# First batch of an mLSTM cell in natural chunks: compact state, fixed banks, gate work and weight joins at other slots

## The chip, the cores and the metric

One NeuronCore of a Trainium2 chip runs the whole kernel. The metric is the device time in microseconds (us) of one execution; the median over the runs is compared. Each engine works through its own queue strictly in order: the tensor engine (PE), VectorE (DVE), ScalarE (ACT), GpSimd (POOL), and SyncE (SP), which here issues every DMA.

## What is computed

An mLSTM cell over 4 batches, 8 heads, 768 tokens and head dimension 40, and behind it a Fourier mix over tokens and features, a layer norm and a ReLU MLP of width 1280.

```python
for t in range(S):                       # mLSTM, per batch and head
    m_new = np.maximum(f_gate[t] + m, i_gate[t])
    f_stab = np.exp(f_gate[t] + m - m_new)
    i_stab = np.exp(i_gate[t] - m_new)
    C = f_stab * C + i_stab * outer(v[t], k[t])
    n = f_stab * n + i_stab * k[t]
    y[t] = sigmoid(o_gate[t]) * (C @ q[t]) / np.maximum(np.abs(n @ q[t]), 1.0)
...
X = np.fft.fft(np.fft.fft(x, axis=1), axis=2)   # x: (batch, 768, 320)
u = x + np.real(X)
un = (u - mean(u)) / np.sqrt(var(u) + 1e-06)
out = u + np.maximum(un @ w_ch1, 0.0) @ w_ch2
```

## The kernel before

The recurrence is done in chunks of 128 tokens, six to a batch. For one chunk and all heads PE computes the scores k.q (`mlstm_scores`, L562), DVE multiplies them by exponential weights W (`mlstm_weigh`, L571), PE adds what the state so far gives (`mlstm_from_state`, L577, with the scaled queries qg of `mlstm_scale_q`, L523) to what the chunk itself gives (`mlstm_from_chunk`, L586), and the state C is decayed and added to (`mlstm_decay` L552 on POOL, `mlstm_to_state` L593 on PE, two copies in `mlstm_gather` L607 on ACT). The heads are copied to SBUF (`mlstm_heads`, L618), turned to rows (`mlstm_turn`, L638) and made into the layer's input x with the output gate `so`, after a tanh (`mlstm_tanh`, L634), in `mlstm_finish` (L743). Batch 0 is done so; batches 1 to 3 are done in half chunks of 64 tokens, from gate data that batch 0's time is used to prepare (`gates_of_halves`, L316, in steps: a maximum `nexts`, L326; copies into `keep`, L334 to 342; the exponentials G, L348; twelve stores M_d, L356; one store G_d, L358; later the exponentials K, L363).

The tokens are not in natural order. In every batch the chunks stand as START says, of which those in BACKWARDS run in reverse, so that chunk c and its partner in PAIRS hold tokens t and 768-t in one partition each. The first token of each half stands in a chunk of its own kind (SPECIAL), for which `mlstm_heads` moves a column.

Then, for a batch: a fold of each pair of row blocks (`mix_fold`, L828; sums and differences for the even and odd parts of both Fourier directions, in the pool `eo`, L837 to 849), products with the sequence tables ds_sb (`mix_seq`, L868; results pz, pzt), with the feature tables dd_sb (`mix_feat`, L932; results pu), the addition to x and its statistics (`mix_add`, L954), the centring of a block by ACT into `uc` (`mix_center`, L982), three transposes (`mix_turn`, L990; put or ph) and the MLP. The tables are loaded by `load_tables` (L464, L465: 1158 KB and 642 KB).

The weights come as 64-bit floats and are turned into fp32 in pieces (`Piece`, L411): take on DVE (L435, L437), convert on ACT (L442 e, L443 m), join on DVE (L449, L451, L455).

The order of all this is written out by hand: `at(slot, phase, fn, args)` enters a call in a plan, and `run` emits the calls by slot and phase (EVAC, FILL, MAIN, FILL_PE are 0, 1, 2, 3). That order is the order of each engine's queue. `plan_mlstm` (L764) places chunk c of batch 0 from slot 3c on, `plan_halves` (L784) the later batches, `plan_mix` (L1028) the mix; `gates` (L147) ends with the places of the gate steps, and the lists `when` and `early` place the weight pieces and the loads.

PSUM has eight banks of 2 KB a partition: ps_m with four (`turn` says which comes next), ps_s with two for scores and ps_h with two for the results ph, pc, px and pt in batch 0; later batches use ps_s and ps_h as two 2-bank tiles.

```python
    early = [(3, mlstm_load, 3), (3, mlstm_load_o, 2), (4, mlstm_load, 4), (5, mlstm_load_decay, 3),
             (5, mlstm_load_decay, 4), (6, None, 2), (7, mlstm_load_o, 3), (7, mlstm_load, 5),
             (11, mlstm_load_decay, 5), (11, mlstm_load_o, 4), (12, load_tables, None),
             (14, mlstm_load_o, 5)]
```

Of the kernel before, what the change touches and what calls it, by code (L numbers as in the profile page):

```python
# [37 lines left out]
COL = (0, L + 1, 2 * L + 2)  # L38
LAST = 2 * L + 1
# [4 lines left out]
BACKWARDS = (2, 4, 5)  # L44
# [13 lines left out]
def kernel(  # L58
# [30 lines left out]
    ps_s, ps_h = (ps_early.enter_context(tc.tile_pool(name=n, bufs=2, space=PSUM)) for n in ("ps_s", "ps_h"))  # L89

    turn = iter("3210321032120312031230123102112310231023102310231")
# [7 lines left out]
    rest = const.tile([L, 2 * L], FP, name="rest")  # L99
# [16 lines left out]
    C_bufs = [const.tile([L, NP, L], FP, name=f"C{n}") for n in range(3)]  # L116
    states = [t.rearrange("p n t -> p (n t)")[:, i * 2 * L:(i + 1) * 2 * L] for t in C_bufs for i in range(2)]
    x_bufs = [const.tile([L, NT, DM + 2], FP, name=f"x{n}") for n in range(2)]

    s_last = const.tile([L, NFF // 2 * L], FP, name="s_last")  # L120
    Cd_bufs = [s_last[:, n * NP * D1:(n + 1) * NP * D1].rearrange("p (n m) -> p n m", m=D1) for n in range(2)]
    hT_bufs = []
# [18 lines left out]
    def idle_products(n, first=False):  # L141
        pw = bank("pi", [L, 2 * L]) if first else ps_s.tile([L, 2 * L], FP, name="pi", tag="ps")
        for i in range(n):
            nc.tensor.matmul(pw, rest[:, 0:L], rest, start=True, stop=True, skip_group_check=True)


    def gates(gp):  # L147
# [3 lines left out]
        hT_bufs.extend(gp.tile([L, NP, L + 1], FP, name=f"h{n}") for n in range(2))  # L151
# [6 lines left out]
        M = gp.tile([L, NT, L], FP, name="M")  # L158
# [6 lines left out]
        ident_b, later_b = (gp.tile([L, L], BF, name=n) for n in ("ident_b", "later_b"))  # L165
# [4 lines left out]
        idle_products(3, True)  # L170
        mlstm_load(0, 0)
        make_identity(nc, ident)
        nc.gpsimd.memset(later_b, 0.0)
# [8 lines left out]
        nc.vector.memset(M[:, 0:2], 0.0)  # L182
        for t in C_bufs:
            nc.scalar.copy(out=t.rearrange("p (two n) t -> p two (n t)", two=2),
                           in_=rest.unsqueeze(1).to_broadcast([L, 2, 2 * L]))
# [8 lines left out]
        for t in hT_bufs + Cd_bufs + alone:  # L194
            nc.gpsimd.memset(t, 0.0)
# [21 lines left out]
        def spread_max(b, c, h0):  # L217
# [5 lines left out]
            k.M.append(bank("pM", [L, NP, L]))  # L223
            nc.tensor.matmul(k.M[-1], ident_b, later_b.unsqueeze(1).to_broadcast([L, NP, L]), start=True, stop=False,
                             skip_group_check=True)
            for h in range(h0, h0 + NP):
                bh = b * H + h
                w, x = (ident[:, bh:bh + 1], M[:, c, :]) if c < 2 else (sel[:, bh:bh + 1], M3[:, c, :])
# [3 lines left out]
        def parts(s):  # L232

            m, rest_ = M[0:BH, s], shift[:, s]
# [5 lines left out]

        def spread_decay(b, c):
            k = chunks[b, c]
            k.G = bank("pG", [L, NP, L])
            for h in range(H):
                r, bh = slice(h % 2 * 64, (h % 2 + 1) * 64), b * H + h
                nc.tensor.matmul(k.G[r, h // 2, :], ident[:, bh:bh + 1].to_broadcast([L, 64]), g[:, c, :],
                                 start=True, stop=True)
# [5 lines left out]
        def decay(s):  # L253
            for c in range(s.start, s.stop):
                nc.scalar.activation(out=g[0:BH, c], in_=M[0:BH, c], func=AF.Exp, scale=-1.0, bias=m_in[:, c])

        def columns(s, j):
            pt = ps_h.tile([L, NT, BH], FP, name="pt", tag="ph")
# [6 lines left out]
        maxima(first, M_INIT)  # L265
        pt = columns(first, 0)
# [34 lines left out]
        def decays():  # L301
            dec = gp.tile([BH, BH // 2, NT], FP, name="dec")
            nc.vector.tensor_tensor(out=dec[:, :, 1:],
                                    in0=g[0:BH, 1:, L - 1].unsqueeze(1).to_broadcast([BH, BH // 2, NT - 1]),
# [1237 lines left out]
```

## Time and profile before

| what | us |
|---|---|
| median of 3 runs (401.59, 401.64, 402.67) | 401.64 |
| profiled execution | 402.01 |
| its span, first to last instruction | 400.3 |
| chunks of batch 0 on PE (from_state of chunks 1, 2, 3, 4, 5) | 18.26, 23.37, 28.39, 34.62, 38.18 |
| last fold of pair 0 of batch 0 ends (DVE) | 47.82 |
| first from_state of batch 1 | 76.19 |

The mean granted PE clock over the span is 0.991. The rest of the span, from 76 to 400, is batches 1 to 3, their mixes and the four MLPs, with PE nearly always busy. A row of the timeline reads: start, length of a group of like instructions, engine and line, operation, output tile and input tiles, sizes, count, and in brackets the idle time of the engine before it and what ended it.

### The profile page before, as it was taken

The page shows a single profiled execution, that of the slowest core. Times are in us where ns is not written, and L with a number is a line of the kernel's source. Part 1 is how long each engine was busy: PE and PEld are TensorE (multiplying, and loading weights), DVE is VectorE, ACT ScalarE, POOL GpSimd, SP SyncE. Part 2 cuts the span into 40 slices and gives each one's busy share as a digit, 9 for nine tenths or more (in the row PEclk, how much of TensorE's full clock was granted, in tenths as well). Part 3 has the DMA queues.
Part 4 walks back from the last instruction along what each step waited for, and adds up shares of the span by engine and source line. Part 5 has one row for each costly group of instructions (what it writes and reads, how often), then busy time and mean ns, then how long its engine had stood idle before and what let it go on. Part 6 is the DMA issues. An engine that isn't in the chain of part 4 may idle for free.

```text
span 400.3 us, 10816 instructions
## 1 busy us (share of the span) xinstructions
PE 384.4 (96%) x4318; PEld 281.2 (70%) x4318; DVE 277.3 (69%) x670; ACT 178.2 (45%) x513; POOL 135.4 (34%) x231
## 2 busy tenths in 40 slices
PE   8999896999889999999999998999999999999996
PEld 6888453556557777755459898856579997556996
DVE  8776963689799546879774688678853785336652
ACT  6978844677533232563542214564440023454000
POOL 6654521676836432263251304562300000020000
PEclk9999996999999999999999999999999999999999
DMA  7987498288776143455000814520000000000000
GB/s 225 295 240 257 104 241 201 73 234 239 239 208 157 61 129 99 155 169 174 7 0 2 215 51 143 182 77 5 0 0 18 18 34 33 2 0 1 34 34 34
DMA packets 22767, 43.97 MB, mean 110 GB/s; under 512 B 3492, under 2 KB 11388, under 8 KB 22588
## 3 DMA queue, kind: packets, MB, share of 16 engines
q1 hardware_dynamic: 22716, 43.27, 36.8%
q8 instruction: 34, 0.56, 0.5%
q14 instruction: 17, 0.14, 0.1%
HBM read 39.16 MB, written 4.10 MB: 108 GB/s over the span
## 4 chain that ended last, share of the span: by engine, by line
PE 73%; DVE 18%; issue 3%; ACT 2%; POOL 2%; DVEq 0%; POOLq 0%; ACTq 0%
PE po L1274 21%; PE pm L1145 14%; PE po L1218 8%; PE pm L1150 5%; PE pu L952 3%; PE ph L549 3%; PE ps L549 3%; PE pm L1082 2%; PE pz L907 2%; DVE so L758 2%; PE put L999 1%; DVE x L761 1%; PE pzt L907 1%; DVE h L1154 1%; PE pM L229 1%
## 5 line engine op out<-in xcount | busy, mean ns | idle before, releaser
L1224 DVE SCALAR_TENSOR_TENSOR x<-po,rstd,x 128x160 f32<-128x160 f32 (+1 forms) x69 | 27.2, 394 | 38.9 <-PE po L1274 36.3
L1154 DVE TENSOR_TENSOR h<-h,pm 128x384 f32<-128x384 f32 x60 | 30.6, 550 | 26.6 <-PE pm L1150 12.1
L545 POOL TENSOR_SCALAR_AFFINE_SELECT W<-W 64x512 f32<-64x512 f32 x36 | 28.1, 780 | 39.3 <-ACT W L520 38.1
L1145 PE MATMUL pm<-uT,w_sb 128*128 128x384 f32 x90 | 37.8, 507 | 0.2 <-DVE uT L1133 0.2
L698 POOL TENSOR_TENSOR C<-C,decB 128x164 f32<-128x164 f32 x33 | 17.9, 542 | 56.2 <-DVE C L705 54.8
L520 ACT ACTIVATE W<-W,colT 128x64 f32<-128x64 f32 x144 | 36.6, 336 | 0.0
L1218 PE MATMUL po<-w_sb,h 128*128 128x320 f32 x120 | 34.1, 435 | 0.0
L1023 POOL TENSOR_TENSOR t<-rstd 128x6 f32<-128x6 f32 x12 | 4.2, 353 | 81.4 <-DVE v L1017 80.9
L530 POOL TENSOR_TENSOR qg<-qk,Gb 128x512 f32<-128x512 f32 x21 | 28.5, 1357 | 7.5 <-DMA Gb<-G_d 7.5
L1082 PE MATMUL pm<-uT,w_sb 128*128 128x384 f32 x80 | 29.9, 509 | 0.0
L1274 PE MATMUL po<-T,S 128*128 128x160 f32 x180 | 28.0, 302 | 1.1 <-DVE x L1224 1.1
L1218 PEld LDWEIGHTS po<-w_sb,h 128*128 128x128 f32 x120 | 22.3, 190 | 9.1 <-issue 0.6
L1274 PEld LDWEIGHTS po<-T,S 128*128 128x128 f32 x180 | 25.4, 190 | 2.7 <-DVE x L1224 1.3
L1150 PE MATMUL pm<-uT,w_sb 64*128 64x384 f32 x120 | 26.3, 511 | 0.4 <-DVE h L1154 0.4
L1274 PE MATMUL po<-w_sb,h 128*128 128x160 f32 x180 | 26.3, 300 | 0.0
L1274 PEld LDWEIGHTS po<-w_sb,h 128*128 128x128 f32 x180 | 25.2, 190 | 1.5 <-DVE x L1224 0.3
L1145 PEld LDWEIGHTS pm<-uT,w_sb 128*128 128x128 f32 x90 | 15.4, 189 | 13.8 <-DVE h L1154 5.9
L1201 ACT ACTIVATE h<-h 128x384 f32<-128x384 f32 x45 | 23.1, 520 | 3.0 <-DVE h L1154 3.0
L988 ACT ACTIVATE uc<-x 128x384 f32<-128x384 f32 x24 | 14.5, 614 | 20.2 <-DVE x L980 20.2
L705 DVE TENSOR_TENSOR C<-C,ps 128x164 f32<-128x164 f32 x33 | 10.5, 317 | 18.0 <-PE ps L549 15.3
L1150 PEld LDWEIGHTS pm<-uT,w_sb 64*128 64x128 f32 x120 | 12.8, 185 | 12.8 <-issue 8.2
L1004 ACT COPY uT<-put 128x384 f32<-128x384 f32 x21 | 9.6, 476 | 26.9 <-PE put L999 26.8
(242 smaller groups left out, 859.5 us busy)
## 6 DMA issues: line engine op xcount, KB each, us to landing
kvt<-in_kv SPq DMA_DIRECT2D x24, 336.0 KB
qk<-in_qkT SPq DMA_DIRECT2D x48, 160.0 KB
raw<-in_w SPq DMA_DIRECT2D x10, 640.0 KB
Gb<-G_d SPq DMA_DIRECT2D x42, 128.0 KB
W<-M_d SPq DMA_DIRECT2D x36, 128.0 KB
so<-in_o SPq DMA_DIRECT2D x24, 160.0 KB
out<-x SPq DMA_DIRECT2D x24, 160.0 KB
ds_sb<-in_dft_s SPq DMA_DIRECT2D x1, 1158.0 KB
```

Source lines behind the costliest of these rows:

```text
L520: nc.scalar.activation(out=k.W[:, h, :], in_=M, func=AF.Exp, scale=-1.0, bias=colT[:, c, 0, b * H + h:b * H + h + 1])
L530: nc.gpsimd.tensor_tensor(out=k.qg[:, :, t], in0=k.qk[:, 0, :, t], in1=k.Gb[:, :, t], op=OP.mult)
L545: nc.gpsimd.affine_select(out=W, in_=W, compare_op=OP.is_ge, fill=0.0, base=base, pattern=[[0, H], [-1 if back else 1, LH]], channel_multi ...
L549: nc.tensor.matmul(out, w, x, start=start, stop=True, skip_group_check=True)
L1082: nc.tensor.matmul(k.pm[i], w1_block(ch, f // 2 * 2 + i), u[2 * ch], start=(ch == 0 and not ahead), stop=(ch == 1 and ahead), skip_group_c ...
L1145: nc.tensor.matmul(bank, w, u, start=start, stop=True, skip_group_check=True)
L1150: nc.tensor.matmul(bank, w1_rest(i)[rows], mlp_u(gr, 1)[rows], start=False, stop=True, skip_group_check=True)
L1154: nc.vector.tensor_tensor(out=h, in0=h, in1=bank, op=OP.add)
L1201: nc.scalar.activation(out=h, in_=h, func=AF.Relu, scale=-1.0)
L1218: nc.tensor.matmul(k.po[m], hidden(gr, f)[:, i * L:(i + 1) * L], w2_sb[:, f, :], start=(f == 0), stop=(f == NFF - 1))
L1224: nc.vector.scalar_tensor_tensor(out=u, in0=po, scalar=k.rstd[:, c:c + 1], in1=u, op0=OP.mult, op1=OP.add)
L1274: nc.tensor.matmul(po, a[:, f], w[:, f], start=start and f == 0, stop=f == half - 1, skip_group_check=True)
```

## The change

- In batch 0 the chunks hold tokens in natural order (reversed in BACKWARDS, now 0, 3 and 4). `_first()` orders the host arrays. The reversed chunks use a mask `later_r`, and the running maxima in the order of the queries are kept beside the natural ones as Mq (`queries()`, three ACT copies). Row 0 of chunks 0 and 1 and of 3 and 4 are exchanged afterwards (`mlstm_rows`, three one-partition copies each).
- The head order of batch 0 becomes that of the others (head h in half h // 4).
- The state of batch 0 is compact: 41 columns for each of four heads in a half of the partitions. `mlstm_from_state` is 8 products of 40x64 in four quadrants of PE for 4 of 128x128. POOL decays it in place in one operation, and DVE adds the chunk's part (`mlstm_add`) where four products with the identity and two ACT copies did it. The decayed copy in s_last goes.
- Banks: heads of batch 0 lie in one tile of two banks (also pt and pzt); pc, px and pM have fixed banks.
- The steps of `gates_of_halves` go from slots 15 to 22 to slots 6 to 23: `nexts` 10, M_d's stores 11, G's exponentials in two halves at 13 and 16. Weight piece 0 is joined in three parts at slots 7, 10 and 13, piece 1 is taken, converted and joined at 16 to 18.5, and piece 2 at 31 to 33 with its load at 15.
- The folds' ends are one addition each instead of an addition and a copy; `eo` has two buffers; the slots of batch 0's folds, sequence and feature products move, and `mix_center` of two blocks stands right behind their `mix_add`.

```diff
-COL = (0, L + 1, 2 * L + 2)
-LAST = 2 * L + 1
+COL = (0, L, 2 * L)
+LAST = 3 * L
...
-BACKWARDS = (2, 4, 5)
+BACKWARDS = (0, 3, 4)
...
-    ps_s, ps_h = (ps_early.enter_context(tc.tile_pool(name=n, bufs=2, space=PSUM)) for n in ("ps_s", "ps_h"))
-
-    turn = iter("3210321032120312031230123102112310231023102310231")
+    ps_s = ps_early.enter_context(tc.tile_pool(name="ps_s", bufs=2, space=PSUM))
+    first_heads_ps = ps_early.enter_context(tc.tile_pool(name="ps_h", bufs=1, space=PSUM)).tile([L, 2, 4 * L], FP, name="hb")
+
+    turn = iter("3210321223102112310231023102310231")
...
+        def queries():
+
+            x, y = M[0:BH, 3], Mq[0:BH, 3:5]
+            nc.scalar.copy(out=y[:, :, 1:], in_=bass.AP(tensor=x.tensor, offset=x.offset + L - 1,
+                                                        ap=[list(x.ap[0]), [L, 2], [-1, L - 1]]))
+            nc.scalar.copy(out=y[:, :, 0:1], in_=M[0:BH, 3:5, 0:1])
+            nc.scalar.copy(out=Mq[0:BH, 5], in_=M[0:BH, 5])
...
-        def decays():
...
+        def decays(step):
+            if step == 0:
+                dec = late["dec"] = gp.tile([BH, BH // 2, NT], FP, name="dec")
+                for c, at_ in ((1, L - 1), (3, 1)):
+                    nc.vector.tensor_tensor(out=dec[:, :, c:c + 2],
+                                            in0=g[0:BH, c:c + 2, at_].unsqueeze(1).to_broadcast([BH, BH // 2, 2]),
+                                            in1=spread_sb[:, L:].unsqueeze(2).to_broadcast([BH, BH // 2, 2]), op=OP.mult)
+            else:
+                pd = late["pd"] = bank("pd", [L, BH // 2, NT - 2])
+                nc.tensor.matmul(pd, spread_sb[:, 0:L], late["dec"][:, :, 1:NT - 1], start=True, stop=True)
...
+            elif step == 20:
+                less, starts, nexts = (late[n] for n in ("less", "starts", "nexts"))
                 nc.vector.tensor_tensor(out=nexts[:, 1:], in0=M[0:BH, 0:NT - 1, L - 1:L], in1=a[:, 1:, 0:1], op=OP.max)
-                nc.gpsimd.tensor_copy(out=starts, in_=M[0:BH, :, 0:L:LH])
                 for out, x in ((less[:, :, 0:1], M[0:BH, :, LH:LH + 1]), (less[:, 0:NT - 1, 1:2], nexts[:, 1:]),
                                (less[:, NT - 1:, 1:2], M[0:BH, NT - 1:, L - 1:L])):
                     nc.gpsimd.tensor_scalar(out=out, in0=x, scalar1=-1.0, scalar2=None, op0=OP.mult)
                 nc.gpsimd.tensor_tensor(out=late["between"], in0=starts, in1=less, op=OP.add)
...
+            elif step == 21:
+                nc.gpsimd.tensor_copy(out=W[:, 0:4:3, LH:LH + 1], in_=late["nexts"][:, 1:5:3])
                 nc.gpsimd.tensor_copy(out=W[:, 4, LH:LH + 1], in_=late["nexts"][:, 5])
             elif step == 2:
-                nc.scalar.activation(out=late["between"], in_=late["between"], func=AF.Exp)
-                for c in range(NT):
-                    for i in range(2):
-                        t = slice(i * LH, (i + 1) * LH)
-                        nc.scalar.activation(out=G[:, c, t], in_=W[:, c, t], func=AF.Exp, scale=-1.0,
-                                             bias=late["starts"][:, c, i:i + 1])
                 nc.sync.dma_start(out=sp_sb, in_=first_heads)
                 for b in range(1, B):
                     for hip in range(2):
...
                             slot = slice(b * H + i * NP, b * H + (i + 1) * NP)
                             nc.sync.dma_start(out=M_d[:, i ^ hip, slot].rearrange("c p t -> p c t"),
                                               in_=W[rows, :, i * LH:(i + 1) * LH])
-                nc.sync.dma_start(out=G_d[:, H:].rearrange("c p t -> p c t"), in_=G[H:BH])
+            elif step in (10, 11):
+                if step == 10:
+                    nc.scalar.activation(out=late["between"], in_=late["between"], func=AF.Exp)
+                for c in range(*(((0, NT // 2), (NT // 2, NT))[step - 10])):
+                    for i in range(2):
+                        t = slice(i * LH, (i + 1) * LH)
+                        nc.scalar.activation(out=G[:, c, t], in_=W[:, c, t], func=AF.Exp, scale=-1.0,
+                                             bias=late["starts"][:, c, i:i + 1])
+                if step == 11:
+                    nc.sync.dma_start(out=G_d[:, H:].rearrange("c p t -> p c t"), in_=G[H:BH])
...
-        at(1, FILL + 0.2, parts, last)
+        at(1, FILL + 0.2, parts, slice(2, 3))
+        at(2, FILL + 0.6, queries)
+        at(4, FILL + 0.2, parts, slice(3, NT))
         at(5, FILL_PE + 2.1, spread_decay, 0, 2)
         for c in range(2, NT):
             for h0 in (0, NP):
                 at(3 * c - 1, FILL_PE + 2, spread_max, 0, c, h0)
         at(2, FILL + 0.5, columns_late)
         at(4, FILL - 0.4, decay_late)
-        at(4, FILL + 0.5, decays)
-        at(5, FILL - 0.5, decays_out)
+        at(4, FILL + 0.5, decays, 0)
+        at(5, FILL_PE + 2.05, decays, 1)
+        at(6, FILL - 0.05, decays_out)
         at(7, FILL + 0.5, clear, fe[:, :, NC:PAD], fe[:, :, PAD + HALF_D - 1:], fe_odd[:, NC:])
-        for n, (s, phase) in enumerate(((15, FILL + 0.75), (16, FILL + 0.75), (18, FILL + 0.75), (19, FILL + 0.75),
-                                        (18, FILL + 0.8), (19, FILL_PE + 0.5), (20, FILL + 0.75),
-                                        (21, FILL_PE + 0.5), (22, FILL + 0.75))):
+        for n, s, phase in ((0, 6, FILL + 0.75), (1, 8, FILL + 0.75), (20, 10, FILL + 0.02), (21, 10, FILL + 0.85),
+                            (2, 11, FILL + 0.75), (10, 13, FILL + 0.3), (4, 14, FILL + 0.8), (11, 16, FILL + 0.1),
+                            (5, 17, FILL_PE + 2.5), (3, 18, FILL + 0.1),
+                            (6, 18, FILL + 0.05), (7, 22, FILL_PE + 4.5), (8, 23, FILL + 0.2)):
             at(s, phase, gates_of_halves, n)
...
-            k.Cd = Cd_bufs[c % 2]
-            for hip in range(2):
-                r, m = slice(hip * 64, hip * 64 + D), slice(hip * 64, hip * 64 + D1)
-                d = decB[r, b * NP:(b + 1) * NP, c].unsqueeze(2).to_broadcast([D, NP, D1])
-                nc.gpsimd.tensor_tensor(out=k.Cd[r], in0=k.C[0][r, :, m], in1=d, op=OP.mult)
+            nc.gpsimd.tensor_tensor(out=halves_state(k.C[1]), in0=halves_state(k.C[0]),
+                                    in1=decB[:, 0:NP, c].unsqueeze(2).to_broadcast([L, NP, D1]), op=OP.mult)
...
-        k.ph = ps_h.tile([L, NP, L], FP, name="ph", tag="ph")
-        if c > 0:
-            for p in range(NP):
-                nc.tensor.matmul(k.ph[:, p, :], k.C[0][:, p, :], k.qg[:, p, :], start=(p == 0), stop=False,
-                                 skip_group_check=True)
+        k.ph = first_heads_ps[:, :, 0:2 * L].rearrange("p hip (m t) -> p hip m t", t=L)
+        for p in range(0, NP, 2) if c > 0 else ():
+            for hip, i in TILES:
+                r, n = slice(hip * 64, hip * 64 + D), (p + i) * D1
+                product(k.ph[half(i), hip, p // 2, :], k.C[0][r, n:n + LH], k.qg[r, p + i, :], p == 0)
 
     def mlstm_from_chunk(b, c):
         k = chunks[b, c]
+        for h in range(H):
+            hip, p = h // NP, h % NP
+            product(k.ph[half(p % 2), hip, p // 2, :], k.v[:, h * D1:h * D1 + LH], k.W[:, h, :], c == 0 and p < 2)
+
+    def mlstm_to_state(b, c):
+        k = chunks[b, c]
+        k.pc = bank("pc", [L, NP, D1], 2 if c > 0 else 1)
         for p in range(NP):
             for hip in range(2):
...
-                for hip in range(2):
-                    r = slice(hip * 64, hip * 64 + D)
-                    nc.tensor.matmul(k.pc[r], ident[:, r], k.Cd, start=False, stop=True, skip_group_check=True)
...
+                h = hip * NP + p
+                product(k.pc[half(hip), p, :], k.k[:, h * D:h * D + LH], k.vw[:, h, :], p == 0)
...
+    def mlstm_heads(b, c):
+        k = chunks[b, c]
+        k.hT = hT_bufs[c % 2]
+        nc.scalar.copy(out=k.hT.rearrange("p (hip m) t -> p hip m t", hip=2), in_=k.ph)
+
...
+    def mlstm_add(b, c):
+        k = chunks[b, c]
+        if c == 0:
+            nc.vector.tensor_copy(out=halves_state(k.C[1]), in_=k.pc)
         else:
-            for r in (slice(hip * 64, hip * 64 + D1) for hip in range(2)) if c == 0 else (slice(0, L),):
-                nc.scalar.copy(out=hT[r, :, 0:L], in_=ph[r])
+            nc.vector.tensor_tensor(out=halves_state(k.C[1]), in0=halves_state(k.C[1]), in1=k.pc, op=OP.add)
...
+    def mlstm_rows(b, c, part):
+
+        spare, x = s_last[0:1, 0:DM], xs[b][0:1, :, 0:DM]
+        if part == 0:
+            nc.scalar.copy(out=spare, in_=x[:, c - 1])
+        elif part == 1:
+            nc.vector.tensor_copy(out=x[:, c - 1], in_=x[:, c])
+        else:
+            nc.scalar.copy(out=x[:, c], in_=spare)
+
+    def plan_mlstm(b):
         for c in range(NT):
-            s = s0 + stride * c
+            s, end = 3 * c, c == NT - 1
             if c > 0:
                 at(s, FILL, mlstm_exp, b, c, 0)
                 at(s + 1, FILL - 0.5, mlstm_exp, b, c, NP)
-                at(s - 1 if c == NT - 1 else s, FILL_PE + (2.05 if c == NT - 1 else 2), mlstm_scores, b, c)
+                at(s, FILL_PE + (3.5 if end else 2), mlstm_scores, b, c)
             at(s, FILL, mlstm_scale_v, b, c)
             at(s if c == 2 else s + 1, FILL + 0.1, mlstm_scale_q, b, c)
-            at(s + 2, FILL, mlstm_decay, b, c)
-            end = c == NT - 1
-            at(s + 1 if end else s + 2, FILL - 0.4 if end else FILL, mlstm_weigh, b, c)
+            at(6 if c == 1 else s + 2, FILL, mlstm_decay, b, c)
+            at(s + 1, FILL + (0.2 if end else -0.4), mlstm_weigh, b, c)
             at(s + 2 if end else s + 3, FILL_PE, mlstm_from_state, b, c)
             at(s + 2 if end else s + 3, FILL_PE + (2 if end else 3), mlstm_from_chunk, b, c)
-            at(s + 3, FILL_PE + 3, mlstm_to_state, b, c)
-            at(s + 3 if end else s + 4, FILL, mlstm_gather, b, c)
-            t, x = ((8, 9), (11, 12), (13, 14), (16, 16.5), (17, 18), (18, 20))[c]
-            at(t, FILL_PE + (2.5 if c < 4 else 1), mlstm_turn, b, c, c < 4)
-            at(x, FILL + 0.05, mlstm_finish, b, c)
+            if not end:
+                at(s + 3, FILL_PE + 3, mlstm_to_state, b, c)
+                at(s + 4, FILL - 0.3, mlstm_add, b, c)
+            at(*((17, FILL_PE + 2.6) if end else (s + 4, FILL - 0.27)), mlstm_heads, b, c)
+            at(*((16, FILL + 0.02) if end else (s + 4, FILL - 0.25)), mlstm_tanh, b, c)
+            t, phase = ((5, 2.5), (8, 2.5), (11, 2.5), (14, 2.5), (16, 0.5), (17, 2.8))[c]
+            at(t, FILL_PE + phase, mlstm_turn, b, c)
+            t, phase = ((6, 0.3), (9, -0.3), (12, -0.3), (15, -0.3), (16.5, 0.4), (18.5, 0))[c]
+            at(t, FILL + phase, mlstm_finish, b, c)
+        for c, part, t, phase in ((1, 0, 7, 0.3), (1, 1, 9, -0.2), (1, 2, 10, -0.1), (4, 0, 16, 0.01), (4, 1, 16.5, 0.45),
+                                  (4, 2, 18, 0)):
...
+                at((17, 18.5, 18.5)[j], FILL + (0.1, 0.2, 0.3)[j], mix_fold, b, p)
+                s, phase = ((17, 3), (19, 3), (22, 4))[j]
+                for i, part in enumerate(((1,), (0,)) if j == 1 else ((0, 1),)):
+                    at(s, FILL_PE + phase + 0.1 * i, mix_seq, b, p, part)
+                at(*((18, FILL_PE + 0.2) if j == 0 else (s, FILL_PE + phase + 0.2)), mix_tail, b, p)
+            else:
+                at(x_done[j] + (b > 1 and j == TG - 1), FILL + 0.5 if b < 2 else FILL_PE + 0.2, mix_fold, b, p)
+            if b > 0 and j == 0:
...
-            at(t, FILL + 0.1, mix_center, b, c)
+            at(*((a, FILL + 0.25) if b == 0 and c in (4, 2) else (t, FILL + 0.1)), mix_center, b, c)
...
-    eo_p = pool("eo", 1)
+    eo_p = pool("eo", 2)
...
-    when = [((2, 0.7), (4, 0.5), (6, 0.6)), ((11, 0.7), (13, 0.7), (22, 0.6)), ((29, 0.7), (30, 0.7), (32, 0.6))]
+    when = [((2, 0.7), (4, 0.5), None), ((16, -0.2), (18, 0.08), (18.5, 0.6)), ((31, 0.7), (32, 0.7), (33, 0.6))]
     when += [((s, 0.7), (s + 1, 0.7), (s + 2, 0.6)) for s in range(33, 52, 3)]
     pieces = w1_pieces + w2_pieces
     for n, (w, p) in enumerate(zip(when, pieces)):
         if n > 2:
             at(when[n - 2][2][0] + 1, FILL + 0.7, p.load)
-        for (s, phase), fn in zip(w, (p.take, p.convert, p.join)):
-            at(s, FILL + phase, fn)
+        for t, fn in zip(w, (p.take, p.convert, p.join)):
+            if t:
+                at(t[0], FILL + t[1], fn)
+    for part, s in enumerate((7, 10, 13)):
...
-             (5, mlstm_load_decay, 4), (6, None, 2), (7, mlstm_load_o, 3), (7, mlstm_load, 5),
-             (11, mlstm_load_decay, 5), (11, mlstm_load_o, 4), (12, load_tables, None),
+             (5, mlstm_load_decay, 4), (7, mlstm_load_o, 3), (7, mlstm_load, 5),
+             (11, mlstm_load_decay, 5), (11, mlstm_load_o, 4), (12, load_tables, None), (15, None, 2),
...
+def _first():
+
+    t = np.arange(S).reshape(NT, L)
+    for c in BACKWARDS:
+        t[c, 1:] = t[c, :0:-1].copy()
+    return t
...
```

## The prediction

> **What bounds the kernel now.** Four views, in this order. The page's busy shares: the tensor engine (PE) is busy 96% of the span, so over most of it any time won must be a shorter PE stream or a PE wait removed. The engines' busy time by stretches (columns: stretch, its length, then busy time with instruction count of PE, PEld, DVE, ACT and POOL, then granted clock, DMA share, GB/s) shows where PE is not full:
>
> ```profile
> PE 384.4 (96%) x4318; PEld 281.2 (70%) x4318; DVE 277.3 (69%) x670; ACT 178.2 (45%) x513; POOL 135.4 (34%) x231
> ```
>
> ```profile
> 20.00:38.00 18.00, 17.96 (x272) 15.03 (x268) 11.69 (x28) 14.22 (x48) 9.93 (x18) 1.00 0.91 274
> 38.00:53.00 15.00, 13.68 (x82) 8.39 (x83) 11.37 (x31) 11.91 (x45) 5.29 (x10) 1.00 0.47 123
> 53.00:64.00 11.00, 7.32 (x32) 3.77 (x31) 9.94 (x25) 6.08 (x14) 2.38 (x3) 0.96 0.94 234
> 64.00:76.00 12.00, 12.00 (x97) 6.71 (x97) 3.52 (x7) 6.92 (x21) 5.62 (x9) 0.75 0.56 143
> ```
>
> In 20 to 38 (the chunks of batch 0) PE is the bound. In 53 to 64 it is idle 3.7 us, and from 64 to 76 it is full but at a granted clock of 0.75. The timeline names the idle time, PE first, then ACT:
>
> ```profile
> 58.20 2.20 PE L1082 MATMUL pm<-uT,w_sb 128*128 128x384 f32 x6
> 63.94 0.90 PE L999 MATMUL ph<-ident,uc 128*128 128x128 f32 x3 [3.54 <-ACT uc L988]
> ...
> 60.97 0.83 ACT L442 ACTIVATE e<-e,ebias 128x640 uint32<-128x640 uint32 x1 [2.83 <-DVE e L435]
> 61.71 0.72 ACT L443 ACTIVATE m<-m 128x640 f32<-128x640 uint32 x1
> 62.33 1.05 ACT L520 ACTIVATE W<-W,colT 128x64 f32<-128x64 f32 x4
> 63.29 0.60 ACT L988 ACTIVATE uc<-x 128x384 f32<-128x384 f32 x1
> ```
>
> PE waits 3.54 us for a centred row block, `uc`, whose ACT instruction stands behind a weight's conversion (e, m), and that one waits for DVE. Last, SP's queue, which issues every load in order, and the DMA rate while the Fourier tables fly:
>
> ```profile
> 28.36 0.33 SPq L464 DMA_DIRECT2D ds_sb<-in_dft_s  x1
> 28.92 0.33 SPq L465 DMA_DIRECT2D dd_sb<-in_dft_d  x1
> 30.32 0.33 SPq L513 DMA_DIRECT2D so<-in_o  x1
> 30.69 0.43 SPq L350 DMA_DIRECT2D sp_sb<-in_heads  x1
> 40.08 4.17 SPq L356 DMA_DIRECT2D M_d<-keep  x12
> ```
>
> ```profile
> 28.00:33.00 5.00, 5.00 (x76) 4.38 (x75) 3.04 (x9) 3.60 (x13) 3.17 (x5) 1.00 1.07 258
> 33.00:38.00 5.00, 4.96 (x72) 4.00 (x69) 2.43 (x7) 4.73 (x15) 3.14 (x9) 1.00 0.88 346
> 38.00:45.00 7.00, 6.08 (x48) 4.11 (x48) 6.30 (x20) 6.17 (x24) 4.32 (x8) 1.00 0.07 20
> ```
>
> The reader is to see that tables and the last output gate (`so`) are issued ten microseconds before the twelve stores of M_d, and that those take SP 4.17 us. The tables are 1158 KB and 642 KB (page, part 6, and its longer form).
>
> **The chunk loop.** Before, from_state of chunks 2 and 3 starts at 23.37 and 28.39 on PE: 5.0 us a chunk. Removed: the four identity products L605 (31.68 to 32.05: 0.38). Smaller: from_state takes 0.98 from its start to that of the scores (28.39 to 29.37); in its compact form it is 16 instructions of 40x64. The trace has 32 of nearly that form for batch 1 (L549, 1.13 for all), so half of that, 0.5 to 0.57, saves 0.4. Bounds: nothing saved to 0.5 saved. The join of C on PE becomes one DVE add (0.32, the row L705 of the same size) and the two ACT copies (0.61) go. That is 5.0 less 0.78, and 0.1 back for from_chunk and the 64-wide keys: 4.3 us a chunk. ACT and DVE have the room (14.2 and 11.7 of 18 busy). POOL does one decay instead of two.
>
> **What eats it.** Three waits, each from the order of the queues.
> (1) The product of the decays, pd, stands in PE's queue after the scores of chunk 1, and its factor `dec` on DVE behind weigh of chunk 1 (1.28). PE waits for it till about 17.8, 1.3 us. From_state of chunk 2 then comes at 23.9.
> (2) `nexts` moves on DVE behind weigh of chunk 3 (ends 27.4 by the walk), the C add (0.32) and a part of a join (0.82): done 28.6. On POOL the operation that reads it stands in front of the scaling of queries of chunk 3. Behind it: 0.22, 0.22, 0.20 and 1.3 to 1.5 (rows L330, L331, L530), so qg is ready at 30.7 where PE is ready at 23.9 + 4.3 = 28.2. PE waits 2.5 us. Chunk 4 starts at 35.0, chunk 5 at 39.3.
> (3) The M_d stores now wait for two POOL copies right behind that qg (31.0), and stand on SP in front of the tables and the last two `so`. 31.0 + 4.17 = 35.2 (sp_sb's 0.43 went first), Gb of chunk 5 1.18 to 36.4, `so` of chunk 4 at 36.4, ds 36.9, dd 37.3, `so` of chunk 5 at 37.4. It lands behind 1.96 MB. At 0.38 MB/us (the slices of 1 us from 33 to 37 show 0.43, 0.39, 0.39, 0.37) that is 5.1 us. From issue to first bytes and for the completion I take 1.9, an estimate: of the loads issued from 0.79 on, only 0.27 MB had moved by 3.0, which at 0.26 MB/us is one microsecond of moving, so 1.2 us of start, and 0.7 for the end (bounds 1.2 to 2.5). The gate lands at 44.3. ACT is ready for its tanh at 39.8, so it stands 4.5 us, and behind it on ACT stand six exponentials of G (0.245 each, from 2.96 for 12), the copy of heads of chunk 5 and the row copy; PE needs those heads for its next transposes.
>
> From there: tanh 0.47, six exponentials 1.5, heads 0.58, transposes 0.5, finish of chunk 5 1.65 with its wait: 49.2. Folds of pair 1 (0.95) and pair 0 (1.7): 51.8, where before the last fold of pair 0 ends at 47.82. The first pu group reaches its end 5.2 later, before 4.93: 57.0 against 52.75, **+4.3**. PE stands still from 42 to 47. The row at 63.94 shows what a stand of 3.54 did: the granted clock is 0.75 over the next 12 us. If that happens here, the groups of products up to pu take 2.2 more: **+6.5**. (The Trainium skill, "TensorE: Matmul & The Clock Gate", section "What's actually happening", has the clock halved after an idle window of about 3.4 us and released after a busy one; by that, the second figure holds, though the stand must fill a free-running window.)
>
> **What it gains after.** mix_center of two blocks moves right behind its mix_add, before the conversion on ACT: the 3.54 of idle goes, if ACT does uc as soon as x is there. The 0.75 clock goes with it: 12 us at 0.75 hold what 9 to 9.4 do at full clock, 2.6 saved. Together **-6.1** between the end of pu and from_state of batch 1 chunk 0 (23.4 us before, 17.3 after). What else is late then: W of that chunk needs M_d, now stored 9 us sooner, and Gb, which needs the G exponentials; by the walk its weights are done at 63.7 where PE needs them at 64.3 or later, so nothing. Bounds of this term: -3.5 (the clock falls all the same) to -6.1.
>
> **At no cost:** eo's second buffer and the one-add fold ends (0.17 to 0.74 each saved, twelve of them, on DVE, while PE runs 0.94 busy behind it); the row exchange (6 one-partition copies, at most 0.5 each by the ops on 128x320 rows; four are on ACT, idle 21% in 20 to 38); weight joins moved into DVE's idle time (0.82 each). If DVE had no cover, each join would cost its 0.82 at the pair folds. Batches 1 to 3 keep their order on every engine, so they are shifted, not changed.
>
> **Sum.** Against the profiled execution, 402.0 (span 400.3): 402.0 + 4.3 - 6.1 = 400.2 at full clock, 402.0 + 6.5 - 6.1 = 402.4 at half; middle 401.3. The median of the runs is 401.64, 0.4 less: 400.9, from 399.8 to 402.0. I take 400.8.
>
> The rule of the queue decides term (3): by the Trainium skill ("DMA: Bandwidth & Descriptors", section "Queues, rings and completion order"), descriptors on each DMA engine are consumed in ring order, so the gate stands behind the tables though it is small. No row here shows a small load overtaking; if it did, the next paragraph's 395 would come out.
>
> **Rivals.**
> A, the forecast: tanh waits for `so` behind the tables. Chance 0.48; own range 398.5 to 402.8.
> B, the gate is not late: the keep copies are not held by POOL, or `so` lands within a microsecond of need. Then the end of pu comes at about 52.2 with the POOL wait and 49.4 without: 52.2 - 52.75 - 6.1 = -6.6, so 395.0, and 392.2 without either wait. For it: POOL is only 55% busy in 20 to 38 and the stores could start earlier if weigh of chunk 3 comes earlier than my 27.4. Against: the order of the queues is fixed. Chance 0.27.
> C, the other side: the tables move at the slow rate. The window 28 to 33 shows 258 GB/s with DMA share 1.07, that is full engines. 1.96 MB at 0.258 is 7.6 us: `so` lands at 46.9, 2.6 later than in A, and the end of pu with it: 403.4 at the middle, 404.5 with the half clock. It decides when `so` lands after about 45.6. For it: in that window the loads in front were the same tables. Against: Gb's 128 KB broadcasts and chunk loads shared it, and they have passed by 37. Chance 0.20.
> D, the change doesn't do what it says: uc of batch 0 is held by something else (the exponentials of batch 1 in front of it), the 3.54 stays, and with the late gate: 406. Chance 0.05.
>
> **Chances.** About 0.3%, 1.2 us, is what can be told from no change. B is faster; A lies across the bound at 400.4 (0.22 faster, 0.20 same, 0.06 slower); C slower; D slower. Faster 0.49, same 0.21, slower 0.30. The range reaches into B to its later half and over C: 393 to 405.
>
> **What would show it.** Right: an ACT idle of about 4.5 us in front of the tanh of the last chunk, released by `so`'s load; M_d's stores starting about 31; a PE wait of 2 to 3 us for qg of chunk 3; the first from_state of batch 1 within 2 us of 74.3; no wait of PE for uc in batch 0. Wrong: `so` of chunk 5 landing before 41, or fold of pair 0 ending before 49 (B), or after 53 (C); a PE wait above 2 us behind pu (D); any change of the span behind that from_state beyond 1 us, which would say that the later batches do not merely shift.

## The result

The changed kernel takes 406.69 us in the median of 4 runs (405.74 to 407.97), the kernel before 402.15 in the same comparison: a ratio of 1.0107, with a 95% interval from 1.0058 to 1.0156. It is slower, and the time lies outside the range that was forecast. The profiled execution took 405.74, its span is 403.6; before, 402.01 and 400.3. Below, medians and ratios are over each kernel's runs in its faster state: two of the ten runs of e1 (407.4 and 408.3) and one of the four of e2 (411.1) lie in a slower one and are left out.

Where the 3.3 us of span come from is read by laying the same events of both traces side by side (PE rows of from_state, DVE rows of the folds and of mix_add; starts in us, of the last fold the end):

| event | before | after | difference | added since the row above |
|---|---|---|---|---|
| from_state of chunk 1 | 18.26 | 20.45 | +2.2 | +2.2 |
| from_state of chunk 2 | 23.37 | 25.04 | +1.7 | -0.5 |
| from_state of chunk 3 | 28.39 | 31.62 | +3.2 | +1.6 |
| from_state of chunk 4 | 34.62 | 39.35 | +4.7 | +1.5 |
| from_state of chunk 5 | 38.18 | 43.09 | +4.9 | +0.2 |
| last fold of batch 0 | 47.82 | 53.44 | +5.6 | +0.7 |
| first mix_add | 52.82 | 59.68 | +6.9 | +1.2 |
| from_state, batch 1 chunk 0 | 76.19 | 77.54 | +1.4 | -5.5 |
| from_state, batch 1 chunk 2 | 92.11 | 95.60 | +3.5 | +2.1 |
| end of the span | 400.3 | 403.6 | +3.3 | -0.2 |

Batch 0 up to its mix loses 6.9, the mix wins 5.5 back, and the start of batch 1 loses 2.1 again. The rows of chunks 4 and 5 hide something: before, the scores of chunk 5 (1.09) lie in front of from_state of chunk 4, after they lie behind it. For like work chunk 3 to chunk 4 loses 2.6 and chunk 4 to chunk 5 wins 0.9. The stretches of the changed kernel (columns as before: PE, PEld, DVE, ACT, POOL busy, clock, DMA share, GB/s):

```profile
20.00:38.00 18.00, 16.08 (x228) 13.43 (x228) 12.85 (x30) 9.26 (x32) 7.40 (x19) 0.83 0.43 120
38.00:53.00 15.00, 12.40 (x133) 8.07 (x132) 11.80 (x33) 11.46 (x41) 6.71 (x10) 0.86 0.54 204
53.00:64.00 11.00, 10.65 (x52) 6.23 (x50) 5.96 (x13) 4.56 (x13) 0.25 (x1) 1.00 0.72 186
64.00:76.00 12.00, 11.48 (x106) 6.29 (x105) 8.87 (x19) 10.06 (x28) 7.84 (x10) 1.00 0.83 210
```

The gap of 53 to 64 and the low clock of 64 to 76 are gone, as was meant. In their place the two earlier stretches have a clock of 0.83 and 0.86, and PE idles in them. The timeline of the changed kernel shows what PE waits for there, then POOL, ACT and SP:

```profile
31.62 1.00 PE L575 MATMUL hb<-qg,C 40*64 40x128 f32 x16 [1.92 <-POOL qg L556]
32.55 2.08 PE L592 MATMUL ps<-qk 40*128 40x128 f32 x16
34.56 1.97 PE L575 MATMUL hb<-W,kvt 128*64 128x128 f32 x16
...
48.28 0.66 PE L632 MATMUL px<-ident,h 128*128 128x128 f32 x4 [2.60 <-ACT h L626]
48.77 2.67 PE L935 MATMUL pz<-ds_sb,fe 128*128 128x386 f32 x4
```

```profile
29.65 0.22 POOL L348 TENSOR_SCALAR less<-nexts 32x5 f32<-32x5 f32 x1 [3.55 <-DVE nexts L345]
...
30.31 1.26 POOL L556 TENSOR_TENSOR qg<-qk,Gb 128x512 f32<-128x512 f32 x1
31.52 0.44 POOL L359 COPY keep<-nexts 32x2 f32<-32x2 f32 x1
31.91 0.18 POOL L360 COPY keep<-nexts 32x1 f32<-32x1 f32 x1
```

```profile
45.86 0.47 ACT L643 ACTIVATE so<-so 128x320 f32<-128x320 f32 x1 [3.42 <-DMA so<-in_o]
```

```profile
25.79 10.22 SPq L368 DMA_DIRECT2D M_d<-keep  x12
36.06 1.09 SPq L533 DMA_DIRECT2D Gb<-G_d  x2
37.25 0.54 SPq L539 DMA_DIRECT2D so<-in_o  x1
37.83 0.43 SPq L491 DMA_DIRECT2D ds_sb<-in_dft_s  x1
38.30 0.42 SPq L492 DMA_DIRECT2D dd_sb<-in_dft_d  x1
38.83 0.38 SPq L539 DMA_DIRECT2D so<-in_o  x1
```

The reader is to see one chain through four queues. POOL idles 3.55 us for nexts with the queries of chunk 3 behind it; PE idles 1.92 for those; and the row after shows the clock: the scores of a chunk, 1.16 elsewhere, take 2.08 (the granted clock from 37 to 38 is 0.50). Behind the queries POOL fixes keep (32.1), only then SP stores M_d (its group of 10.22 us is mostly the wait), then come Gb, the tables and, last, the gate of chunk 5, issued at 38.83 and landed 7.0 us later. ACT stands 3.42 us for it, PE 2.60 for the heads behind it, and the next products again run at half clock (2.67 for what took 1.46 before, behind a wait of 0.74). The row of the kernel before:

```profile
41.99 1.46 PE L919 MATMUL pz<-ds_sb,fe 128*128 128x386 f32 x4
```

In the start of batch 1 it is DVE and ACT:

```profile
72.77 1.94 DVE L475 SCALAR_TENSOR_TENSOR e<-raw,e 128x640 uint32<-128x640 uint32 x1
74.63 0.81 DVE L478 SCALAR_TENSOR_TENSOR m<-raw,m 128x640 f32<-128x640 uint32 x1
75.48 1.24 DVE L482 TENSOR_TENSOR w_sb<-m,e 128x640 f32<-128x640 f32 x1
76.75 0.83 DVE L460 TENSOR_SCALAR e<-raw 128x640 uint32<-128x640 uint32 x1
77.50 0.94 DVE L462 TENSOR_SCALAR m<-raw 128x640 uint32<-128x640 uint32 x1
78.36 0.31 DVE L705 TENSOR_TENSOR C<-C,ps 128x164 f32<-128x164 f32 x1
```

```profile
78.73 0.69 PE L575 MATMUL ps<-qk 40*64 40x64 f32 x32 [0.51 <-DVE C L705]
...
80.05 0.68 PE L575 MATMUL ph<-kvt,W 64*64 64x41 f32 x32 [0.31 <-ACT warm L741]
```

Piece 2's join and piece 3's take stand in front of the add that PE waits for; piece 3's conversion (ACT, 77.6 to 79.2) stands in front of the ACT copy that the second row waits for. In the kernel before, piece 2 was worked on almost wholly inside the 3.54 us in which PE stood anyway, 60.4 to 63.9 (taken from 60.48, joined from 61.83):

```profile
61.83 0.83 DVE L449 SCALAR_TENSOR_TENSOR e<-raw,e 128x640 uint32<-128x640 uint32 x1 [0.49 <-ACT e L442]
...
63.43 0.82 DVE L455 TENSOR_TENSOR w_sb<-m,e 128x640 f32<-128x640 f32 x1
```

### The profile page after: what moved, and what is told of

Read it like the earlier page. It is cut to its first block, busy times and chain, and to the rows that moved or that the text cites. A ratio compares the mean times of both kernels' runs of the same rounds, so it can differ in the third digit from the quotient of the medians.

```text
span 403.6 us, 10881 instructions
## 1 busy us (share of the span) xinstructions
PE 385.5 (96%) x4342; PEld 281.3 (70%) x4342; DVE 280.8 (70%) x680; ACT 175.0 (43%) x505; POOL 134.7 (33%) x235
## 4 chain that ended last, share of the span: by engine, by line
PE 65%; DVE 11%; issue 2%; POOL 1%; ACT 1%; DVEq 0%; POOLq 0%
PE po L1297 20%; PE pm L1168 15%; PE po L1241 8%; PE pm L1173 5%; PE ph L575 3%; PE pu L968 3%; PE ps L575 2%; PE pm L1105 2%; PE pz L923 2%; DVE so L758 1%; PE put L1015 1%; PE pzt L923 1%; DVE C L705 1%; DVE h L1177 1%; PE pm L1096 1%
## 5 line engine op out<-in xcount | busy, mean ns | idle before, releaser
L1168 PEld LDWEIGHTS pm<-uT,w_sb 128*128 128x128 f32 x90 | 15.4, 189 | 13.9 <-DVE h L1177 5.9
L1105 PEld LDWEIGHTS pm<-uT,w_sb 128*128 128x128 f32 x80 | 14.0, 189 | 10.9 <-issue 3.4
```

The costliest lines, as they stand in the source:

```text
L1105: nc.tensor.matmul(k.pm[i], w1_block(ch, f // 2 * 2 + i), u[2 * ch], start=(ch == 0 and not ahead), stop=(ch == 1 and ahead), skip_group_c ...
L1168: nc.tensor.matmul(bank, w, u, start=start, stop=True, skip_group_check=True)
```

## The experiments

Times are medians; ratios are to the kernel before in the same comparison.

**e1: nexts and the keep copies early.**

```diff
-(20, 10, FILL + 0.02), (21, 10, FILL + 0.85),
+(20, 7, FILL + 0.75), (21, 8, FILL + 0.85),
```

> The step that makes nexts (and the POOL operations behind it) at slot 7 for 10, the two keep copies at 8 for 10. Theory (the queue waits set the end of batch 0): the 1.9 us wait of PE for the scaled queries of chunk 3 goes, and with it the half clock that the trace shows behind it from 31.6 to 38 (chunk 3 takes 7.7 us on PE for 4.6): 1.9 + 3.1 = 5.0 us less, about 401.7; the last tanh still waits some 3.4 us for its gate, since stores, tables and gate all move up together. Rival (the landing of the tables or work on DVE sets the end of batch 0, the PE wait is covered): within 1 us of the changed kernel, above 405.

402.74 us, ratio 1.0019 (0.9996 to 1.0042): 4.0 less than the changed kernel. The POOL wait of PE becomes 0.61 (for the state, another releaser), from_state of chunk 3 to chunk 4 takes 4.6, the wait of PE for the last heads stays at 2.57. The theory holds. The gain is smaller than the 5.0 expected: 0.6 of a new wait remains, and from_state of chunk 5 to the first mix_add takes 17.7 for 16.6, with a granted clock of 0.77 for 0.86 in 38 to 53.

**e2: the last gate in front of the tables.**

```diff
-(12, load_tables, None), (15, None, 2), (14, mlstm_load_o, 5)]
+(11, mlstm_load_o, 5), (12, load_tables, None), (15, None, 2)]
```

> The load of the last output gate in front of the two tables. Theory: the 3.4 us that ACT stands for it go; PE waits for the last heads 0 to 0.5 for 2.6, the half clock from 48 to 52 goes too (about 1.5): 3.5 to 4.5 us less, about 402.7. Rival (the tables' own landing sets the products that follow, the gate is covered): PE waits for ds_sb in its place, gain under 1 us.

405.30, ratio 1.0084 (1.0067 to 1.0101): 1.4 less, not 3.5 to 4.5. The waits for the gate and for the last heads are gone. A wait of 1.09 for a fold on DVE takes their place, and the products behind it still run at half clock (2.94). In the profiled execution PE also ran slowly for longer at the start (groups of pM take 2.05 and 1.91 for 1.13 and 1.05, though the granted clock reads 1.00 there), and from_state of chunk 1 comes at 22.67. Counted from that row, the first mix_add comes 36.8 us later, against 39.2 in the changed kernel. But 1.5 of these 2.4 lie between from_state of chunks 3 and 4 (6.2 for 7.7), where PE waited for the queries as before (1.91) and the half clock only lasted less long; the rows behind from_state of chunk 4 give the edit 0.9.

**e3: both edits.**

> Both edits. Theory: the two add up, 8 to 9 us less, about 398, faster than before by 1%. Rival (each wait covers the other, or PE reaches the products before the tables are there): not more than the larger of the two alone.

400.47, ratio 0.9968 (0.9946 to 0.9990): 6.2 less than the changed kernel and faster than before. That is clearly more than either alone, so neither wait covers the other. It is also more than the sum of the two (5.4), but this excess lies within the spread.

**e6: PE kept busy in its wait.**

```diff
+        at(11.9, FILL_PE, idle_products, 3, rest, 2)
```

> The changed kernel with three idle products of 128x256 on PE (1.5 us at full clock) in the 1.9 us in which it waits for the scaled queries of chunk 3; nothing waits for them but PE itself. Theory (that wait costs 1.9 us by itself and 3 more by the half clock from 31.6 to 38): chunk 3 takes 4.6 us on PE for 7.7, the granted clock of 20 to 38 is 1.00 for 0.83, and the time falls by up to 3 us, to about 403.7; but the gate lands no sooner, so the wait for the last heads grows by what is won, and the net may be 0 to 1.5. Rival (the clock falls with the lack of work over a longer stretch, or there is no tie to this wait): clock and time as in the changed kernel.

407.68, ratio 1.0120 (1.0075 to 1.0164): no gain, and the profile shows why:

```profile
29.61 1.46 PE L142 MATMUL pi<-rest 128*128 128x256 f32 x6
31.69 0.67 PE L576 MATMUL hb<-qg,C 40*64 40x128 f32 x16 [0.62 <-POOL qg L557]
32.29 1.16 PE L593 MATMUL ps<-qk 40*128 40x128 f32 x16
...
48.80 1.12 PE L633 MATMUL px<-ident,h 128*128 128x128 f32 x4 [5.26 <-ACT h L627]
```

The scores take 1.16 again and chunk 3 takes 4.6 us (31.69 to 36.29): the low clock hung on the wait of 1.92. But PE then waits 5.26 for the last heads where it waited 2.60: the gate lands at 46.4 whatever PE does, since its issue hangs on POOL's copies and SP's queue (it landed at 45.9 without the idle products).

**e14: e6 and e2 together.**

> The two edits of e2 and e6 together: the last gate loaded in front of the tables, and three idle products in PE's wait for the queries of chunk 3. Each alone won at most 1.2. Theory (e6 won nothing because the gate's landing, fixed by SP's queue, set the end; with the gate out of the way the full clock in chunk 3 is worth its 3 us): 2.5 to 3.5 us less than e2, about 402.5. Rival (the half clock behind that wait lies beside other waits and is worth nothing): as e2, 405.5.

403.40, ratio 1.0034 (1.0016 to 1.0052), 1.9 less than e2 though e6 alone won nothing: what the full clock is worth shows once the gate is out of the way. A little less than expected; the queries of chunk 5 now cost PE 1.17.

**e4: piece 2 back at its slots.**

```diff
-((31, 0.7), (32, 0.7), (33, 0.6))]
+((29, 0.7), (30, 0.7), (32, 0.6))]
```

> Weight piece 2 taken, converted and joined at slots 29, 30, 32 as before, for 31, 32, 33. Theory (the 1.2 us that the first chunk of batch 1 loses against before come from weight work standing in DVE's queue in front of the state's add): about 1.2 us less, 405.5, and the distance between the first two from_state of batch 1 back from 8.4 to 7.2. Rival (that loss comes from the loads or from PE's own instruction supply): no change, and the distance stays.

406.65, ratio 1.0134 (1.0105 to 1.0163): no change in time, so the 1.2 expected did not come. The distance between the first two from_state of batch 1 is 7.2 again (79.17 to 86.36), so that distance does come from the weight work, but the first of them comes 1.6 later. The conversion now stands on ACT in front of the copy that PE needs:

```profile
72.67 0.55 PE L1015 MATMUL ph<-ident,uc 128*128 128x128 f32 x3 [1.48 <-ACT uT L1020]
```

The work of piece 2 must lie somewhere; in both places it lies on PE's path.

**e5: the kernel before with the centring moved, alone.**

```diff
-            at(t, FILL + 0.1, mix_center, b, c)
+            at(*((a, FILL + 0.25) if b == 0 and c in (4, 2) else (t, FILL + 0.1)), mix_center, b, c)
```

> The kernel before with one edit alone: the centring of two blocks right behind their mix_add, as in the change. The prediction's term: the 3.5 us that PE waits for uc go and the lower clock behind them, 6.1 us less, about 395.8. Theory now (the weight's conversion that stood in that wait must be done somewhere: it comes to lie in front of the first chunks of batch 1 on DVE and ACT, where the changed kernel loses 2.1): 3.5 to 4.5 us less, about 398, with some 2 us more than before between the first two or three from_state of batch 1. Rival (the wait for uc only covers the wait for batch 1's weights or for the conversion): under 1 us.

397.93, ratio 0.9889 (0.9855 to 0.9923): 4.3 less than before. PE's wait for uc is gone and the clock of 64 to 76 is 1.00; a wait of 1.46 for uT behind the conversion has come instead, in front of batch 1 rather than between its chunks (those stand 7.2 apart).

**e12: the same, with piece 2 taken, converted and joined at 22, 23 and 30.**

> The kernel before with the centring moved and piece 2 taken at 22, converted at 23 and joined at 30 for 29, 30, 32. Theory (what e5 gives back is 1.5 us of PE waiting for uT behind the conversion on ACT): that wait goes, 1.0 to 1.5 us less than e5, 396.6. Rival (another wait takes its place): as e5, 397.9.

396.45, ratio 0.9849 (0.9831 to 0.9868). The wait for uT is gone and the 5.8 us won are nearly the 6.1 of the prediction's term. This one line of the change beats both kernels, with piece 2 taken and converted where DVE and ACT wait for pu and joined right behind the last mix_add; nothing else of the change is in it.

**e8: e3 with piece 2 taken and converted at 20 and 23.**

> Both edits of the third run, and weight piece 2 taken and converted at slots 20 and 23 (where DVE waits 4 us for pu) and joined at 33 as in the change. Theory (0.9 us of DVE and 1.5 of ACT leave the start of batch 1, where they stand in front of the state's add and of uT): 1 to 1.5 us less than the third run, about 399.2. Rival (the 2.1 us lost there are not from this piece but from the loads or the instruction supply): as the third run, 400.5.

399.94, ratio 0.9940 (0.9918 to 0.9963): 0.5 less than e3, within the spread. The distance of the first two from_state stays at 8.4: taking and converting piece 2 is not what delays the add.

**e9: e8 with the order of the start mended.**

```diff
-            for h in range(H):
+            for h in (0, 4, 1, 5, 2, 6, 3, 7):
-        at(4, FILL + 0.5, decays, 0)
+        at(4, FILL + 0.05, decays, 0)
-(1, 8, FILL + 0.75), (20, 7, FILL + 0.75), (21, 8, FILL + 0.85),
+(1, 7, FILL - 0.3), (20, 7, FILL - 0.5), (21, 7, FILL - 0.2),
```

> The run before this with three more edits: the products that spread G in an order of heads that alternates the two halves of the array (0, 4, 1, 5, ...), as before the change; the factor of the decays made in front of the scaled queries of chunk 1 on DVE; nexts, the keep copies and their fixes moved ahead of weigh of chunk 2 (slot 7). Theory (the start lost 2.2 us to these: two spreads at 1.58 for 1.09, a PE wait of 0.8 for the decays, a wait of 0.6 for the state): 2 us less again, about 397.3. Rival (the start is set by ACT or by loads): under 0.5.

399.38, ratio 0.9916 (0.9887 to 0.9944), 0.6 less than e8 for the 2 expected. The start is mended: from_state of chunk 1 at 19.54, chunk 3 at 28.99, chunk 5 at 37.41 (20.48, 30.35 and 38.77 in e8). But the first mix_add comes only 0.5 sooner (53.53 for 54.04): PE then waits 1.09 for the fold of pair 2, as in e8, and in this execution its clock fell behind that wait (2.32 for products that took 1.57 in e8).

**e11: e9 with piece 2's join at slot 30.**

> The mended order (nexts early, gate first, spreads and decays in order, piece 2 taken and converted at 20 and 23) with piece 2's join at slot 30, right behind the last mix_add, for 33. Theory (the 2.4 us of join stand in DVE's queue in front of the state's add of batch 1 chunk 0, which PE waits for): the first two from_state of batch 1 stand 7.2 apart for 8.4, 1.2 us less than e9: 398.2. Rival (that distance has another cause, loads or PE's supply of instructions): as e9, 399.4.

398.56, ratio 0.9921 (0.9886 to 0.9956): against e9 the time is unclear, from 397.4 to 403.3 over ten runs. The five runs with a granted clock of 0.999 or 1.000 take 397.4 to 397.9, the five with 0.983 to 0.990 take 399.2 to 403.3, so the spread goes with the clock. The rows are clear: the first two from_state of batch 1 stand 7.2 apart (73.47 and 80.66), so the join was what delayed the add. In the profiled execution PE waited 1.69 for the queries of chunk 5 and lost its clock behind it (0.66 in 38 to 53).

**e13: e11 with the fold of pair 2 at slot 16.**

> e11 with the fold of pair 2 of batch 0 in front of the finish of chunk 4 on DVE, slot 16, as before the change, for 17 behind it. Theory (the chunk loop won 2 us but PE then waits 1.1 for that fold and runs its products at half clock): 1 to 1.5 us less than e11, 397. Rival (the tables land only then, or the finish of chunk 4 that is pushed back costs as much): as e11 or slower.

398.70, ratio 0.9914 (0.9884 to 0.9945), as e11, without the 1 to 1.5 expected. The kernel folds pair 2 before row 0 of chunks 3 and 4 has been exchanged, so that exchange is left out of the fold: the early place isn't to be had in this form. What holds the fold back in the change is the exchange: it needs the rows of chunk 4. The first mix_add came 14.9 after from_state of chunk 5 (16.1 in e9), so the tie is worth at most 1.2 us, and 0.4 against e8 (15.3), where the clock didn't fall.

## Why the prediction was wrong

**Right: the chain through the queues.** PE's wait for the queries of chunk 3 was put at 2.5 and measured 1.92; the M_d stores at 31.0 to 35.2, measured 32.1 to 36.0; the gate's landing 6.9 after its issue, measured 7.0; ACT's wait at 4.5, measured 3.42, because ACT came 2.6 later than forecast (42.4 for 39.8) and the gate 1.6 later. PE's stand in front of the last heads was put at 5 (42 to 47) and measured 2.60, because PE came to it only at 45.7. e1, e2, e3 and e14 show that this chain sets the end of batch 0, so rivals B and D are refuted. C is not what happened either, though by the prediction's own marks it is C's case (the gate landed at 45.86, after 45.6, and the last fold ended at 53.44, after 53). The gate was issued 1.4 later than forecast and took 7.0 from there, as A has it, not the 9.5 of C's slow rate; from 40 to 45 the DMA moved 380 to 435 GB/s. No small load overtook the tables.

**Right: the centring.** Forecast -6.1, measured -5.5 in the trace, alone -4.3 (e5), and -5.8 with piece 2 moved out of its way (e12).

**Mis-sized: the loss of batch 0.** Forecast 4.3 to 6.5, measured 6.9. Two terms were short. The start was put at 0.5 later (from_state of chunk 2 at 23.9) and was 1.7; the spread of G had been costed at its old duration, and it takes 1.58 for 1.09, twice, because four heads, eight instructions, in a row now write the same half of the array (e9 has 1.09 again with the two halves alternating as before). And the half clock was counted only behind the last wait, with even odds: it already came behind the first, from 31.6 to 38.5. e6 and e14 show that tie. A chunk took 4.6 at full clock, not 4.3: adding the chunk to the state takes 0.55 for the old 0.30. The compact from_state cost 0.60 for the 0.5 to 0.57 forecast, which is luck: the row that was halved for it, 1.13, stands in the stretch with a clock of 0.75 (the same 32 instructions take 0.67 at full clock) and has 64 columns for 128.

**Wrong: "Batches 1 to 3 keep their order on every engine, so they are shifted, not changed", and weight joins at no cost.** This is the step that fails: 2.1 us were lost between chunk 0 and chunk 2 of batch 1; without them the median would lie inside the range (404.6). The prediction took the 3.54 us wait as pure loss and did not ask where the work that had caused it would go. Removed from the wait, that work came to lie in front of the state's add (after, e8, e9) or of uT (e4, e5). e11 and e12 take and convert piece 2 where DVE and ACT wait for pu and join it right behind the last mix_add, and the loss of 1.2 from the join is gone. About 0.9 of the 2.1 is something else, and its cause stays open. Chunk 1 to chunk 2 of batch 1 takes 9.6 us for 8.7, and PE has a gap of 0.63 in it that the trace puts down to no releaser ("issue"):

```profile
90.49 1.56 PE L1105 MATMUL pm<-uT,w_sb 128*128 128x384 f32 x4 [0.63 <-issue]
```

The gap, 0.23 to 0.96 long, stands behind the third or fourth of the same eight instructions in every variant that has as many PE instructions as the change. It is absent before, in e5 and e12, and also in e6 and e14 (8.74 and 8.92 from chunk to chunk), which differ there by six idle instructions 60 us earlier. This points to the place in PE's stream rather than to data, but that is not shown; whether it is the supply of instructions no run here tells.

**The sum.** 6.9 - 5.5 + 2.1 - 0.2 is 3.3 of span. Of the profiled times' 3.7, the other 0.4 lie outside the span: 2.14 for 1.71 before. The 4.5 between the medians include two runs of 407.5 and 408.0 whose traces were not kept, at the same granted clock (0.987) as the two of 405.7 and 405.9; a slow start as in e2 would explain them, but that is not shown. The middle of the forecast was -0.7 of span (-6.1 against 4.3 to 6.5): the 4.0 between it and the measured 3.3 are 1.5 from batch 0, 0.6 from the centring and 2.1 from batch 1, less 0.2. The range was too narrow because it held only the first loss against the gain.

## What to carry to other kernels

When an edit takes away a wait, list the work that was being done during that wait: it becomes late next, and e12 against e5 is what placing it is worth. When a step moves to an earlier slot, follow what it waits for through every in-order queue that it now heads: here one small operation on POOL set a store, a table load and a gate on SP. Two waits in series hide each other: e6 alone won nothing and e2 alone 1.4, while e14 and e3 show what lies under them.

## What the runs showed of the hardware

A short wait was enough to halve PE's clock: 1.92 us in the changed kernel (the next 6.9 us at half), 1.69 in e11; after a wait of 1.09 it fell in e3 and not in e8. The mean granted clocks of the runs lie mostly near 1.000, 0.996, 0.991, 0.987: steps of 0.0043 of 400 us, which is 1.7 us lost each time. That fits the Trainium skill, "TensorE: Matmul & The Clock Gate", section "What's actually happening", in that the clock is judged and granted in free-running windows of about 3.4 us and halved, since half of 3.4 is 1.7; its idle window of the same length isn't what these waits filled, and here the measurement decides. So part of the spread of a kernel's times is how many such windows it falls into (e11's ten runs), but not all of it: the four runs of the changed kernel differ by 2.2 us at one granted clock.

The copy of one row on DVE, 0.31 us in the changed kernel with POOL idle beside it, took 1.63 beside two POOL operations (e3; DVE, then POOL):

```profile
27.84 1.63 DVE L770 COPY x<-x 1x320 f32<-1x320 f32 x1
```

```profile
27.34 0.73 POOL L562 TENSOR_TENSOR vw<-kvt,colT 128x328 f32<-128x328 f32 x1
28.04 1.26 POOL L556 TENSOR_TENSOR qg<-qk,Gb 128x512 f32<-128x512 f32 x1
```

It ended 0.17 after the second did. By the Trainium skill, "SBUF — State Buffer", section "🔬 SBUF: two separate sides", GpSimd shares a pair of ports with VectorE operations that run in a two-port mode or have two SBUF inputs, and whichever starts first holds it for its whole instruction while the other is blocked. The rows agree, if this copy is such an operation, which they don't show.
